# An odd unit's magnitudes ahead of the sigmoids, in the ticks that have exponentials

## The chip, the cores and the metric

The kernel runs on one core of a Trainium2 chip. The metric is device time in microseconds (us) of one execution. The engines are PE (TensorE: matmuls, with PEld for its weight loads), DVE (VectorE), ACT (ScalarE), POOL (GpSimd) and SP (SyncE, which here issues the DMAs). Each runs its own instructions in the order of the program and meets the others at semaphores.

## What is computed

Inducing-point attention over x (4 x 12480 x 128, 32 inducing rows), and then a feed-forward layer of 2048 columns with a rational function as its activation:

```
h   = mab(I, x)                      # softmax(I x^T / sqrt(C)) x
x2  = mab(x, h)                      # softmax(x h^T / sqrt(C)) h
h   = x2 @ w_in
P   = a[0] + a[1] * h + a[2] * h**2 + a[3] * h**3
Q   = 1.0 + |b[0]| * |h| + |b[1]| * h**2
out = (P / (Q + 1e-06)) @ w_out
```

## The kernel before

A first part reads x once and makes the pooled attention of the first of the 4 batches; then the weights are turned from 64-bit to 32-bit words. The main part, `fast_ticks`, walks over 832 units. A unit is one column block of 480 tokens (26 a batch) and two of the 16 slices of 128 hidden columns, so a unit's arrays are 128 x 960. One tick t stands for one unit, and the units form pairs (an even one and the odd one behind it). The later batches' attention is cut into small steps, which `side` puts between the ticks by a budget per engine when the program is built.

Q is quadratic in |h|, and with a shifted and scaled h the quotient becomes a sigmoid of a logarithm. A unit goes through these stages, with the names that the profile shows:

- `first` (L729), a tick ahead: two matmuls of 480 columns into PSUM (`hp<-at,st`). There are three `hp` buffers, so a unit's matmuls wait until the unit three before it has been read for the last time.
- The magnitude. For an even unit DVE takes it (`u<-hp`, L807). For an odd one ACT does, with an Abs (`u<-hp,all`, L821). Both halves lie in one tile `u` of 128 x 1920, so that ACT's later functions take a pair at once. There are 7 such tiles.
- The numerator's first factors: on DVE for an odd unit (`l<-u,all,hp`, L810, in the tick after it, reads the Abs), on POOL and then DVE for an even one (`l<-u,all`, L813, and `l<-hp,all,l`, L802).
- ACT: Ln over the pair (`u<-u`, L816), later Sigmoid over the pair (`u<-u,all`, L818).
- The product with the sigmoid: on DVE for an even unit (`l<-l,all,u`, L799, in tick t for unit t - 11), on POOL for the odd one behind it (`u<-l,all`, then `l<-u`, L831 and L832). POOL's first instruction writes into the half of `u` that DVE's product has just read.
- `second` (L744), 12 ticks behind: four matmuls with w_out into one PSUM tile `po`, and after eight units a column block leaves over `oT`.

Ln and Sigmoid need different tables on ACT, and a change of table is an instruction of its own (ACT_TABLE_LOAD). So the ticks run in groups of eight: with turn = (t - 6) mod 8, four Ln of four pairs in turns 0 to 3 and the four sigmoids of the same pairs in turns 4 to 7. Exponentials of the later batches' attention (`e<-e,nmc` and `a<-a`) are gathered in a queue, `exp_q`, and `run_act` lets them out in turn 4 alone, where the tables change anyhow. The table in use there for Ln is exchanged for one with the exponential first, so that such a turn has two loads: one ahead of the exponentials, one ahead of the sigmoids.

The order in which instructions are written in `fast_ticks` is the order on each engine (`InOrder`, L147, pins it). In a tick it is: matmuls of earlier and next units, DVE's and POOL's work, ACT's waiting side jobs and exponentials (`run_act`, L814), the Ln or Sigmoid of the turn, the Abs if the tick is odd (L819 to L821), and the side steps. The Abs of the odd tick behind turn 4 thus stands behind the group's second sigmoid.

Of the kernel before, what the change touches and what calls it, by code (L numbers as in the profile page):

```python
# [13 lines left out]
AF = mybir.ActivationFunctionType  # L14
# [30 lines left out]
class Params:  # L45


    def __init__(self, nc, pool, moe_a, moe_b):
        self.nc, self.pool, self.n = nc, pool, 0
        self.all = pool.tile([P, 128], F32, name="all")  # L50
        ab = pool.tile([P, 6], F32, name="ab")
        nc.sync.dma_start(out=ab[:, 0:4], in_=moe_a.rearrange("(o n) -> o n", o=1).broadcast_to((P, 4)))
        nc.sync.dma_start(out=ab[:, 4:6], in_=moe_b.rearrange("(o n) -> o n", o=1).broadcast_to((P, 2)))
        self.a = [ab[:, i:i + 1] for i in range(4)]
        self.b0 = self.abs(ab[:, 4:5])
        self.b1 = self.abs(ab[:, 5:6])
# [116 lines left out]
class Kernel:  # L173
# [50 lines left out]
    def run_act(self, exps=True):  # L224
        while self.act_q and self.act_q[0][0] < self.tick:
            _, do, done = self.act_q.pop(0)
            do()
            done.append(1)
        if exps:
            for do in self.exp_q:  # L230
                do()
            self.exp_q = []

    def run_jobs(self, spare):

        for job in list(self.jobs):
            gen, since, (ticks, v, g) = job
            if self.tick - since < ticks:
                continue
            if v > spare["v"] or g > spare["g"]:  # L240
                break
            spare["v"] -= v
            spare["g"] -= g
            need = next(gen, None)
            if need is None:
                self.jobs.remove(job)
            else:
                job[1:] = self.tick, need
# [528 lines left out]
    def fast_ticks(self, units):  # L777

        V, A, G, p = self.nc.vector, self.nc.scalar, self.nc.gpsimd, self.params
        n = len(units)
        at = lambda t: units[t] if 0 <= t < n else None
        self.first(units[0])
        for t in range(n + 13):
            u, last, d = at(t), at(t - 1), at(t - 11)
            group, turn = divmod(t - 6, 8)
            w = at(8 * group + 2 * (turn % 4))
            late = at(t - 12) and at(t - 12).key[2] == 0  # L790
            if late:
                self.fetched = self.fetch()
            if at(t - 12) and not late:
                self.second(at(t - 12))
            if at(t + 1):
                self.first(at(t + 1))
            if t % 2:
                if d:
                    V.scalar_tensor_tensor(out=d.g, in0=d.g, scalar=p.k3, in1=d.u, op0=ALU.add, op1=ALU.mult)  # L799
                    self.last_on_pool(at(t - 10), d)  # L800
                if last:
                    V.scalar_tensor_tensor(out=last.g, in0=last.h, scalar=p.k2, in1=last.g, op0=ALU.add, op1=ALU.mult)  # L802
            else:
                if u:
                    u.pair = self.mp.tile([P, 2, 2, BT], F32, tag="u", name=f"u{u.i}", bufs=7)
                    u.u = u.pair[:, 0]
                    V.tensor_scalar(out=u.u.bitcast(I32), in0=u.h.bitcast(I32), scalar1=0x7FFFFFFF, scalar2=None, op0=ALU.bitwise_and)  # L807
                if last:
                    last.g = self.new(last, "l", 14)
                    V.scalar_tensor_tensor(out=last.g, in0=last.u, scalar=p.k1, in1=last.h, op0=ALU.add, op1=ALU.mult)  # L810
                if u:
                    u.g = self.new(u, "l", 14)
                    G.tensor_scalar(out=u.g, in0=u.u, scalar1=1.0, scalar2=p.k1, op0=ALU.mult, op1=ALU.add)  # L813
            self.run_act(turn == 4)  # L814
            if w and turn < 4:
                A.activation(w.pair, w.pair, AF.Ln, bias=LAM, scale=LAM)  # L816
            elif w:
                A.activation(w.pair, w.pair, AF.Sigmoid, bias=p.lnc, scale=-2.0)  # L818
            if u and t % 2:  # L819
                u.u = last.pair[:, 1]  # L820
                A.activation(u.u, u.h, AF.Abs, bias=p.back, scale=1.0)  # L821
            self.side(u or units[-1])
            if late:
                self.second(at(t - 12))
        self.fetch()

    def last_on_pool(self, d, before):

        G, p = self.nc.gpsimd, self.params
        if d:  # L830
            G.tensor_scalar(out=before.u, in0=d.g, scalar1=1.0, scalar2=p.k3, op0=ALU.mult, op1=ALU.add)  # L831
            G.tensor_tensor(out=d.g, in0=before.u, in1=d.u, op=ALU.mult)  # L832
# [87 lines left out]
class Unit:  # L920


    def __init__(self, b, n, q):
        self.key, self.i = (b, n, q), f"{b}_{n}_{q}"


# [22 lines left out]
```

## Time and profile before

| | us |
|---|---|
| median of 3 runs | 2594.55 (2594.13 to 2599.68) |
| the profiled execution | 2594.75 |
| its span in the profile | 2592.9 |
| TensorE clock granted, mean | 0.966 of full speed |
| DMA queue 1, share of 16 engines' span | 17.6% |

Times in the profile are counted from the span's start. A page or a group's row gives busy time, mean duration and the idle time of the engine just before the group's instructions, with what released it. A row of the timeline gives start, duration, engine, line, instruction (what it writes, an arrow, what it reads) and, in brackets, the idle time before it and the releaser; neighbours of one kind are merged (x2), with their common duration. A row of the chain gives start, length and engine of a piece. All work is issued through the one helper at L157, so instructions are told apart by their tiles' names, in which buffer numbers are left out.

### The profile page before, as it was taken

What the parts mean: (1) busy time and instruction counts of PE and PEld (TensorE: products, weight loads), DVE (VectorE), ACT (ScalarE), POOL (GpSimd) and SP (SyncE); (2) the same over time, 40 slices, a digit from 0 to 9 for tenths busy, and PEclk for the clock granted to TensorE, in tenths of its full rate; (3) what the DMA queues carried; (4) which work ended last, traced back from release to release, by engine and by line L of the source; (5) the groups of instructions that cost most, each with busy time, mean ns of one, the idle gap of its engine ahead of it and who ended that gap; (6) DMA issues with size and microseconds to landing.
All of it is one profiled execution on the core that took longest, in us unless ns stands there. A gap on an engine that the chain in (4) does not pass through costs nothing.

```text
span 2592.9 us, 24006 instructions
## 1 busy us (share of the span) xinstructions
PE 2249.2 (87%) x7508; PEld 1233.8 (48%) x7508; DVE 2210.1 (85%) x2318; ACT 2244.9 (87%) x1590; POOL 2011.4 (78%) x1420
## 2 busy tenths in 40 slices
PE   7798888999899789989988898888888888888887
PEld 4544444555454355544544465444435434434333
DVE  6578778899899889899898888988889888888886
ACT  1488889989889999888899998899999999999996
POOL 2267767888787788888687887887888887888887
PEclk9699989999999999999999999999999999999999
DMA  7222201211222012112321131011101001000000
GB/s 251 73 62 78 73 27 52 71 50 31 70 83 80 19 31 76 50 48 63 92 55 48 35 88 38 16 42 31 46 27 50 27 20 38 20 22 24 17 17 17
DMA packets 117357, 133.68 MB, mean 52 GB/s; under 512 B 13544, under 2 KB 115816, under 8 KB 117224
## 3 DMA queue, kind: packets, MB, share of 16 engines
q1 hardware_dynamic: 117224, 132.06, 17.6%
q8 instruction: 64, 1.05, 0.2%
q14 instruction: 69, 0.57, 0.1%
HBM read 80.89 MB, written 25.56 MB: 41 GB/s over the span
## 4 chain that ended last, share of the span: by engine, by line
DVE 32%; PE 22%; ACT 19%; POOL 18%; issue 6%; DMA 1%; SPq 1%; DVEq 0%; POOLq 0%; ACTq 0%
DVE l L157 21%; ACT u L157 13%; POOL l L157 13%; PE po L157 13%; DVE u L157 7%; ACT L157 4%; POOL u L157 4%; PE hp L157 3%; PE ph L157 2%; PE pd L157 2%; DVE oT L157 1%; POOL a L157 1%; SPq L157 1%; DVE asm L157 1%; DMA x<-x_t 1%
## 5 line engine op out<-in xcount | busy, mean ns | idle before, releaser
L157 PE MATMUL po<-l,w_out 128*128 128x480 f32 x3328 | 1545.8, 592 | 188.4 <-POOL l L157 183.6
L157 PEld LDWEIGHTS po<-l,w_out 128*128 128x128 f32 x3328 | 607.3, 194 | 773.0 <-issue 419.7
L157 POOL TENSOR_TENSOR l<-u 128x960 f32<-128x960 f32 x416 | 932.2, 2241 | 34.7
L157 ACT ACTIVATE u<-u 128x1920 f32<-128x1920 f32 x416 | 739.8, 1799 | 193.2 <-DVE l L157 143.0
L157 PE MATMUL hp<-at,st 128*128 128x480 f32 x1664 | 742.7, 529 | 98.3 <-DVE l L157 91.1
L157 ACT ACTIVATE u<-u,all 128x1920 f32<-128x1920 f32 x416 | 766.1, 1887 | 1.2
L157 POOL TENSOR_SCALAR u<-l,all 128x960 f32<-128x960 f32 x416 | 445.5, 1071 | 392.8 <-DVE l L157 363.4
L157 DVE SCALAR_TENSOR_TENSOR l<-l,all,u 128x960 f32<-128x960 f32 x416 | 597.8, 1437 | 105.7 <-ACT u L157 105.3
L157 DVE SCALAR_TENSOR_TENSOR l<-hp,all,l 128x960 f32<-128x960 f32 x416 | 503.5, 1210 | 121.8 <-POOL l L157 114.0
L157 POOL TENSOR_SCALAR l<-u,all 128x960 f32<-128x960 f32 x416 | 555.6, 1336 | 64.7 <-DVE u L157 63.7
L157 DVE TENSOR_SCALAR u<-hp 128x960 int32<-128x960 int32 x416 | 477.0, 1147 | 75.6 <-PE hp L157 74.3
L157 PEld LDWEIGHTS hp<-at,st 128*128 128x128 f32 x1664 | 312.6, 193 | 431.3 <-issue 325.3
L157 DVE SCALAR_TENSOR_TENSOR l<-u,all,hp 128x960 f32<-128x960 f32 x416 | 500.3, 1203 | 0.3 <-ACT u L157 0.3
L157 ACT ACTIVATE u<-hp,all 128x960 f32<-128x960 f32 x416 | 434.7, 1045 | 36.4 <-PE hp L157 36.3
L157 ACT ACT_TABLE_LOAD x234 | 300.2, 1283 | 4.9 <-PEq L942 0.7
L157 PE MATMUL ph<-x,eT 120*32 120x129 f32 x832 | 105.8, 280 | 9.0 <-DMA x<-x_t 6.3
L157 PEld LDWEIGHTS pd<-HT,xTb 128*120 128x120 f32 x832 | 103.3, 198 | 9.7 <-DMA xTb<-x_c 4.3
L157 PE MATMUL pd<-HT,xTb 128*120 128x32 f32 x832 | 100.5, 277 | 5.2 <-DMA xTb<-x_c 4.1
L157 PEld LDWEIGHTS ph<-x,eT 120*32 120x32 f32 x832 | 88.9, 112 | 28.0 <-issue 21.5
L157 DVE COPY oT<-po 128x480 f32<-128x480 f32 x104 | 67.3, 647 | 21.6 <-PE po L157 21.3
L157 PE MATMUL po<-at,st 128*128 128x480 f32 x104 | 80.7, 776 | 0.0
L157 PE MATMUL pc<-xTa,ind 128*128 128x480 f32 x156 | 72.2, 566 | 1.9 <-DMA xTa<-x_c 1.9
(84 smaller groups left out, 621.6 us busy)
## 6 DMA issues: line engine op xcount, KB each, us to landing
x<-x_t SPq DMA_DIRECT2D x104, 240.0 KB, 3.5
xTb<-x_c SPq DMA_DIRECT2D x104, 240.0 KB, 2.8
at<-hl SPq DMA_DIRECT2D x416, 60.0 KB, 2.0
out<-oT SPq DMA_DIRECT2D x104, 240.0 KB, 2.0
xTa<-x_c SPq DMA_DIRECT2D x78, 240.0 KB, 2.8
xTw<-x_c SPq DMA_DIRECT2D x5, 960.0 KB, 10.3
raw<-w_in SPq DMA_DIRECT2D x4, 480.0 KB, 14.2
raw<-w_out SPq DMA_DIRECT2D x5, 384.0 KB, 5.9
```

Source lines behind the costliest of these rows:

```text
L157: ins = call(*args, **kw)
```

## The change

`run_act` now says whether it let exponentials out. If it did, the Abs of the next tick's odd unit is issued at once, behind the exponentials and ahead of the turn's sigmoid; the odd tick then leaves it out. Everywhere else the Abs stays where it was. The instruction itself moves into a method.

```
-        if exps:
-            for do in self.exp_q:
-                do()
+        todo = self.exp_q if exps else []
+        for do in list(todo):
+            do()
+        if todo:
             self.exp_q = []
+        return bool(todo)
...
-            self.run_act(turn == 4)
+            if self.run_act(turn == 4) and at(t + 1):
+                self.magnitudes(at(t + 1), u)
             if w and turn < 4:
                 A.activation(w.pair, w.pair, AF.Ln, bias=LAM, scale=LAM)
             elif w:
                 A.activation(w.pair, w.pair, AF.Sigmoid, bias=p.lnc, scale=-2.0)
-            if u and t % 2:
-                u.u = last.pair[:, 1]
-                A.activation(u.u, u.h, AF.Abs, bias=p.back, scale=1.0)
+            if u and t % 2 and u.u is None:
+                self.magnitudes(u, last)
...
+    def magnitudes(self, u, partner):
+        u.u = partner.pair[:, 1]
+        self.nc.scalar.activation(u.u, u.h, AF.Abs, bias=self.params.back, scale=1.0)
```

(`Unit` also sets `u` to None at first.)

On ACT, this is the place in the first batch where the exponential of a scores tile (`a_3`) stands in turn 4. The names give tile, column block and first slice: `hp_8_3` are the matmuls of block 8's odd unit, and `u_8_2` is the tile of its pair.

```order
 L157 ACT_TABLE_LOAD
 L157 ACTIVATE a_3_1576<-a_3_1576 120x1024
+L157 ACTIVATE u_8_2_1841<-hp_8_3_1838,all 128x960
 L157 ACT_TABLE_LOAD
 L157 ACTIVATE u_7_0_1658<-u_7_0_1658,all 128x1920
 L157 ACTIVATE u_7_2_1706<-u_7_2_1706,all 128x1920
-L157 ACTIVATE u_8_2_1841<-hp_8_3_1838,all 128x960
 L157 ACTIVATE u_7_4_1741<-u_7_4_1741,all 128x1920
 L157 ACTIVATE u_7_6_1771<-u_7_6_1771,all 128x1920
```

The Abs has passed one table load and two sigmoids. The number of rows and of table loads on ACT is the same; 26 Abs move in this way.

DVE's rows stand in the old order, but what they wait for changes. This is the group after that one, behind its turn 4, with the waits of each row; `l_9_3` is the product that reads the moved Abs, `l_8_2` the one that reads the second sigmoid.

```order
-L157 TENSOR_SCALAR u_9_4_1995<-hp_9_4_1970 128x960 [waits PE_49]
-L157 SCALAR_TENSOR_TENSOR l_9_3_1997<-u_9_2_1957,all,hp_9_3_1954 128x960 [waits Activation_49]
-L157 SCALAR_TENSOR_TENSOR l_8_2_1845<-l_8_2_1845,all,u_8_2_1841 128x960
-L157 SCALAR_TENSOR_TENSOR l_9_4_1999<-hp_9_4_1970,all,l_9_4_1999 128x960 [waits Pool_49]
+L157 TENSOR_SCALAR u_9_4_1995<-hp_9_4_1971 128x960 [waits PE_49]
+L157 SCALAR_TENSOR_TENSOR l_9_3_1997<-u_9_2_1957,all,hp_9_3_1954 128x960
+L157 SCALAR_TENSOR_TENSOR l_8_2_1845<-l_8_2_1845,all,u_8_2_1841 128x960 [waits Activation_49]
+L157 SCALAR_TENSOR_TENSOR l_9_4_1999<-hp_9_4_1971,all,l_9_4_1999 128x960 [waits Pool_49]
```

The wait for ACT has passed from the product with the Abs to the product with the second sigmoid. The product with the first sigmoid stands ahead of both and waits for ACT before and after.

More of the change, by code (lines that the diff above doesn't have):

```diff
@@ L923, in __init__ @@
     def __init__(self, b, n, q):
-        self.key, self.i = (b, n, q), f"{b}_{n}_{q}"
+        self.key, self.i, self.u = (b, n, q), f"{b}_{n}_{q}", None
 def kernel(x, inducing, moe_w_in, moe_w_out, moe_a, moe_b):
```

## The prediction

> **What bounds the kernel now.** The page's first part, and the chain that ended last by engine:
>
> ```profile
> PE 2249.2 (87%) x7508; PEld 1233.8 (48%) x7508; DVE 2210.1 (85%) x2318; ACT 2244.9 (87%) x1590; POOL 2011.4 (78%) x1420
> DVE 32%; PE 22%; ACT 19%; POOL 18%; issue 6%; DMA 1%; SPq 1%; DVEq 0%; POOLq 0%; ACTq 0%
> ```
>
> No engine is full and the chain changes hands all the time: the kernel is a ring of five engines that release one another, and a share of busy time does not say what a delay costs. So I read next who waits for whom in the groups of instructions that the change touches (busy us, mean ns, then idle time before them and its releaser):
>
> ```profile
> L157 ACT ACTIVATE u<-u 128x1920 f32<-128x1920 f32 x416 | 739.8, 1799 | 193.2 <-DVE l L157 143.0
> L157 ACT ACTIVATE u<-u,all 128x1920 f32<-128x1920 f32 x416 | 766.1, 1887 | 1.2
> L157 DVE SCALAR_TENSOR_TENSOR l<-l,all,u 128x960 f32<-128x960 f32 x416 | 597.8, 1437 | 105.7 <-ACT u L157 105.3
> L157 DVE SCALAR_TENSOR_TENSOR l<-u,all,hp 128x960 f32<-128x960 f32 x416 | 500.3, 1203 | 0.3 <-ACT u L157 0.3
> L157 ACT ACTIVATE u<-hp,all 128x960 f32<-128x960 f32 x416 | 434.7, 1045 | 36.4 <-PE hp L157 36.3
> L157 ACT ACT_TABLE_LOAD x234 | 300.2, 1283 | 4.9 <-PEq L942 0.7
> ```
>
> The rows are, in order, the Ln, the sigmoid, DVE's product with the sigmoid's output (L799), DVE's product with the odd unit's magnitudes (L810), the odd Abs and the table loads. Two rows decide the case. DVE waits 105.3 us for **sigmoids** and 0.3 us for **Abs** in the whole run. The change gives DVE the Abs sooner and the first two sigmoids later.
>
> How often: 234 loads are one at the start, 103 for Ln (the first group needs none), 104 for sigmoids, and so 26 for exponentials. The program order moves 26 Abs, one a place. Now one such place in order of time, ACT first (start, duration, instruction):
>
> ```profile
> 328.18 1.04 ACT L157 ACTIVATE u<-hp,all 128x960 f32<-128x960 f32 x1
> 329.24 1.28 ACT L157 ACT_TABLE_LOAD   x1
> 330.53 1.10 ACT L157 ACTIVATE e<-e,nmc 128x960 f32<-128x960 f32 x1
> 331.64 1.28 ACT L157 ACT_TABLE_LOAD   x1
> 332.94 3.68 ACT L157 ACTIVATE u<-u,all 128x1920 f32<-128x1920 f32 x2
> 336.53 1.04 ACT L157 ACTIVATE u<-hp,all 128x960 f32<-128x960 f32 x1
> 337.47 3.67 ACT L157 ACTIVATE u<-u,all 128x1920 f32<-128x1920 f32 x2
> ```
>
> The Abs that moves is the one at 336.53; it goes to 331.6, ahead of the load at 331.64. The other engines there (the row at 339.88 is the product with the second sigmoid):
>
> ```profile
> 329.20 0.96 PE L157 MATMUL hp<-at,st 128*128 128x480 f32 x2
> 334.87 1.22 DVE L157 SCALAR_TENSOR_TENSOR l<-l,all,u 128x960 f32<-128x960 f32 x1 [2.18 <-ACT u L157]
> 336.19 1.07 POOL L157 TENSOR_SCALAR u<-l,all 128x960 f32<-128x960 f32 x1 [3.81 <-DVE l L157]
> 339.88 1.71 DVE L157 SCALAR_TENSOR_TENSOR l<-l,all,u 128x960 f32<-128x960 f32 x1
> 337.36 0.66 PE L157 MATMUL hp<-at,st 128*128 128x480 f32 x2 [3.45 <-DVE l L157]
> ```
>
> DVE stands 2.18 us for the first sigmoid, and POOL (3.81) and PE (3.45) stand for DVE. Everything is stopped behind that one sigmoid. The chain through this group, from the load to the group's third Ln (a piece of DVE, PE or POOL each time the releaser changes), and that Ln's own wait:
>
> ```profile
> 331.64 1.28 ACT L157
> 332.94 1.91 ACT u L157
> 334.87 1.23 DVE l L157
> 336.19 1.08 POOL u L157
> 337.34 2.23 POOL l L157
> ...
> 353.20 1.13 DVE l L157
> 354.42 2.76 ACT u L157 x2
> ```
> ```profile
> 354.42 1.80 ACT L157 ACTIVATE u<-u 128x1920 f32<-128x1920 f32 x1 [2.52 <-DVE l L157]
> ```
>
> It goes from the sigmoid over DVE, POOL, PE and DVE back into ACT, and ACT waits 2.52 us at its end. So a late first sigmoid is handed round the ring to the next group.
>
> **The change part by part.** *Removed:* the Abs behind the second sigmoid. Started at 336.53, it held the next sigmoid until 337.47, so 0.94 us: two ACTIVATEs overlap by 0.10. *Added:* the same Abs behind the exponentials. It overlaps the exponential in the same way, so it can start 1.00 after the exponential's start at 330.53; the next table load follows an Abs by 1.06 (328.18 to 329.24), while it followed the exponential by 1.11 (330.53 to 331.64). First and second sigmoid are therefore late by 1.00 + 1.06 - 1.11 = **0.95 us**; the third gets 0.94 back and is on time. No load, no DMA and no instruction is added or dropped: the order shows the same 234 loads, and ACT issues no DMA that would be moved past. The Ln's and DVE's changed semaphore lists I put at nothing: a wait whose event is long past shows no idle time (the sigmoids' 1.2 us over 416).
>
> *The added wait:* the Abs reads the `hp` of the next odd unit. In the place above its matmuls end at 329.20 + 0.96 = 330.16, before the exponential's end, and Abs does not wait. That holds at 19 of 26. At 7 the matmuls end after the exponential; the first and the last of the 7:
>
> ```profile
> 150.17 0.63 ACT L157 ACTIVATE a<-a 120x512 f32<-120x512 f32 x1
> 151.45 0.97 PE L157 MATMUL hp<-at,st 128*128 128x480 f32 x2
> ...
> 1422.80 1.09 ACT L157 ACTIVATE e<-e,nmc 128x960 f32<-128x960 f32 x1
> 1424.70 0.97 PE L157 MATMUL hp<-at,st 128*128 128x480 f32 x2
> ```
>
> There 152.42 - 150.80 = 1.62 and 1425.67 - 1423.89 = 1.78 (1.77 unrounded); between them lie 1.43, 1.01, 0.04, 0.21 and 1.41, together 7.49 us. Behind the waiting Abs the whole of ACT is queued: load, four sigmoids, next Abs; and DVE, POOL and PE wait for the first of those. How soon Abs follows such matmuls:
>
> ```profile
> 348.07 0.97 PE L157 MATMUL hp<-at,st 128*128 128x480 f32 x2
> 349.14 1.06 ACT L157 ACTIVATE u<-hp,all 128x960 f32<-128x960 f32 x1 [1.78 <-PE hp L157]
> ```
>
> 0.10 us behind their end. So at a late place the first sigmoid is late by the wait + 0.10 + 1.06, less the 0.01 that the load already stood behind the exponential: wait + 1.15.
>
> *What hides it:* nothing, where DVE already waits for that sigmoid. It does so at all 26; the first and the last:
>
> ```profile
> 154.04 1.22 DVE L157 SCALAR_TENSOR_TENSOR l<-l,all,u 128x960 f32<-128x960 f32 x1 [1.50 <-ACT u L157]
> ...
> 2194.66 1.22 DVE L157 SCALAR_TENSOR_TENSOR l<-l,all,u 128x960 f32<-128x960 f32 x1 [2.73 <-ACT u L157]
> ```
>
> The 26 waits run from 1.18 to 3.58 us and make 63.3 of the 105.7. The second sigmoid, late as well, is needed by DVE only at 339.88 in the place above, 3.3 us after its old end of 332.94 + 3.68 = 336.62: covered. The gain, a sooner Abs, is at most the 0.3 us of its row.
>
> *The sum:* 19 x 0.95 = 18.1; 7 x 1.15 + 7.49 = 15.5; together **33.6 us**, to which the 0.3 at most is a gain I neglect. Of this, how much is handed on? At 21 of the 26 places the chain leaves ACT for DVE at the first sigmoid, as above: all of it. At 5 it stays on ACT for all four sigmoids, as here:
>
> ```profile
> 306.78 5.61 ACT u L157 x4
> ...
> 316.00 1.08 POOL u L157
> ```
>
> There only the third sigmoid's lateness counts for certain, and the rest if DVE has no slack; bounds per place are 0.01 and 0.95, 4.7 us for the five. I take the full value, the one that the 21 others have: DVE stood for the first sigmoid at these five too, so its own row of work starts that much later. The profiled execution took 2594.75 us (span 2592.9 and 1.85 around it), 0.2 from the median of 2594.55. So 2594.75 + 33.6 = **2628**; 2623.6 with the five at their low bound.
>
> A rule to weigh here. From the end of the exponential at 331.63 to the sigmoid at 332.94 the rows have 1.31 us, the load and next to nothing. The Trainium skill (ScalarE: Activation LUTs, What ACT_TABLE_LOAD costs) gives a switch about 1283 ns for the load and about 1380 ns more for a drain, 2.66 us in all; were there such a drain behind the exponential, Abs could run in it, and the sum would keep only the late matmuls. The load's length agrees; the drain is not in these rows, and the rows decide.
>
> **The rivals.** *Handed on in part* (10%). DVE is 85% busy, so between two exchanges it could catch up; the chain's 6% of "issue" may hide slack that I count as none. Half of 33.6 is 16.8: 2611.6. Against it: POOL's and PE's waits above are caused by DVE's.
>
> *ACT is the bound* (6%). Its 87% is the highest that counts pure work. The moved Abs leaves ACT's work the same, and the third sigmoid moves by 0.01, or by wait + 0.21 where the matmuls are late: 19 x 0.01 + 7 x 0.21 + 7.49 = 9.2, so 2603.9. Against it are the 193.2 us in which ACT stands before Ln. (The Trainium skill, Perfetto Trace Analysis, Identifying the Most-Contended Engine, takes the engine of the highest occupancy for the one to work on and warns of matmul time; by that rule this rival would be the forecast. Here the chain has ACT at 19%, DVE at 32%.)
>
> *Not slower: it is swallowed before the Ln* (6%). ACT idles up to some 2.5 us before the group's third Ln. If that wait is ended by work which does not come from the first sigmoid, then lateness below it vanishes: 2594.8, and at most 0.3 less. It decides where the idle time exceeds 0.95, or the wait + 0.21 at a late place, and where the chain into that Ln does not pass the first sigmoid. Against it: in the group shown it does pass.
>
> *Worse* (4%). Late groups make later `hp` matmuls late against the exponentials, so that more than 7 places wait: were all 26 to wait the 1.07 us that the 7 average, 26 x (1.15 + 1.07) = 57.7, so 2652. Against it: in the place shown the matmuls end 1.5 us ahead of the exponential, more than one place adds.
>
> That the move does not take place is excluded by the order.
>
> **How the numbers follow.** The forecast has 74%. 0.2%, or 5.2 us, is about what a measurement of this kernel can tell from no change. Of the swallowed case I put 2% to faster and 4% to within 0.2%; all others are slower, 94%. The range runs from below the half case, 2610, to 2640, some way into the last one; outside stay ACT as the bound, the swallowed case and most of the worst, under 16%, and some error of the forecast itself.
>
> **What would show it.** In the changed profile: 26 Abs between exponential and load, the Abs group's idle time behind `hp` up from 36.3 by some 8 us; DVE's idle time before the sigmoid products up from 105.7 by about 30, that of POOL and PE behind DVE at these places by about 1 us each; the first sigmoid 2.3 us (before: 1.3) behind the exponential's end; ACT busy unchanged at 2245; the Ln's idle time up by some 20. The forecast is wrong if the span grows by much less than DVE's wait for sigmoids does (swallowed, or handed on in part), or if the first sigmoid comes later than by 0.95 us at most places (worse).

## The result, and the profile after

The changed kernel takes 2632.9 us (median of 4 runs, 2631.97 to 2633.79), the one before 2596.02 beside it: a ratio of **1.0140, 95% interval 1.0123 to 1.0158**, so 1.4% slower, 36 us of 2596 (32 to 41 by the interval). The forecast was 2628, with a range of 2610 to 2640.

The same groups as before, on the page of the changed kernel (busy us, mean ns, then idle time before them and its releaser):

```profile
PE 2264.0 (86%) x7508; PEld 1241.0 (47%) x7508; DVE 2205.2 (84%) x2318; ACT 2246.7 (85%) x1590; POOL 2010.1 (76%) x1420
L157 ACT ACTIVATE u<-u 128x1920 f32<-128x1920 f32 x416 | 739.9, 1799 | 213.9 <-DVE l L157 153.1
L157 DVE SCALAR_TENSOR_TENSOR l<-l,all,u 128x960 f32<-128x960 f32 x416 | 593.9, 1428 | 138.2 <-ACT u L157 137.8
L157 DVE SCALAR_TENSOR_TENSOR l<-u,all,hp 128x960 f32<-128x960 f32 x416 | 500.0, 1202 | 0.3 <-ACT u L157 0.3
L157 ACT ACTIVATE u<-hp,all 128x960 f32<-128x960 f32 x416 | 435.0, 1046 | 55.4 <-PE hp L157 53.4
```

ACT does the same work (2244.9 before, 2246.7 now). The product with the Abs still waits 0.3 us in the whole run: the change gave DVE nothing sooner that it had been waiting for. The product with the sigmoid waits 137.8 us for ACT instead of 105.3: 32.5 us more. Who waited for that product in turn, in the view of the waits (total us, times, longest), first in the kernel before and then in the changed one:

```profile
POOL u L157 <- DVE l L157: 363.4, 252, 4.0
PE hp L157 <- DVE l L157: 91.1, 77, 3.6
```
```profile
POOL u L157 <- DVE l L157: 398.9, 254, 5.8
PE hp L157 <- DVE l L157: 124.8, 81, 5.0
```

POOL has 35.5 us more, PE 33.7. The place that the prediction showed, now in order of time, first ACT, then DVE, POOL and PE:

```profile
335.52 1.10 ACT L157 ACTIVATE e<-e,nmc 128x960 f32<-128x960 f32 x1
336.52 1.04 ACT L157 ACTIVATE u<-hp,all 128x960 f32<-128x960 f32 x1
337.58 1.28 ACT L157 ACT_TABLE_LOAD   x1
338.88 7.25 ACT L157 ACTIVATE u<-u,all 128x1920 f32<-128x1920 f32 x4
```
```profile
340.81 1.22 DVE L157 SCALAR_TENSOR_TENSOR l<-l,all,u 128x960 f32<-128x960 f32 x1 [2.30 <-ACT u L157]
342.12 1.07 POOL L157 TENSOR_SCALAR u<-l,all 128x960 f32<-128x960 f32 x1 [3.93 <-DVE l L157]
343.30 0.74 PE L157 MATMUL hp<-at,st 128*128 128x480 f32 x1 [3.81 <-DVE l L157]
```

From the exponential's start to the first sigmoid it is 338.88 - 335.52 = 3.36 us; before it was 332.94 - 330.53 = 2.41. The difference is the 0.95 that the sum used. The first of the seven places with late matmuls:

```profile
148.39 0.63 ACT L157 ACTIVATE a<-a 120x512 f32<-120x512 f32 x1
150.74 1.06 ACT L157 ACTIVATE u<-hp,all 128x960 f32<-128x960 f32 x1 [1.72 <-PE hp L157]
...
149.68 0.97 PE L157 MATMUL hp<-at,st 128*128 128x480 f32 x2
```

Here the Abs stands 1.72 us for PE, and the load and all four sigmoids stand behind it.

### The profile page after: what moved, and what is told of

The parts are those of the page before. It is cut to its first block, busy times and chain, and to the rows that moved or that the text cites. A ratio compares the mean times of both kernels' runs of the same rounds, so it can differ in the third digit from the quotient of the medians.

```text
span 2631.4 us, 23981 instructions
## 1 busy us (share of the span) xinstructions
PE 2264.0 (86%) x7508; PEld 1241.0 (47%) x7508; DVE 2205.2 (84%) x2318; ACT 2246.7 (85%) x1590; POOL 2010.1 (76%) x1420
## 4 chain that ended last, share of the span: by engine, by line
DVE 30%; PE 27%; POOL 18%; ACT 17%; issue 5%; DMA 2%; SPq 1%; POOLq 0%; DVEq 0%; ACTq 0%
DVE l L157 20%; PE po L157 16%; POOL l L157 12%; ACT u L157 12%; DVE u L157 6%; PE hp L157 4%; POOL u L157 4%; ACT L157 4%; PE ph L157 3%; PE pd L157 2%; DVE oT L157 1%; SPq L157 1%; PE pc L157 1%; POOL a L157 1%; DVE asm L157 1%
## 5 line engine op out<-in xcount | busy, mean ns | idle before, releaser
L157 PEld LDWEIGHTS po<-l,w_out 128*128 128x128 f32 x3328 | 614.6, 196 | 775.4 <-issue 430.8
L157 ACT ACTIVATE u<-u 128x1920 f32<-128x1920 f32 x416 | 739.9, 1799 | 213.9 <-DVE l L157 153.1
L157 PE MATMUL hp<-at,st 128*128 128x480 f32 x1664 | 743.9, 529 | 132.5 <-DVE l L157 124.8
L157 DVE SCALAR_TENSOR_TENSOR l<-l,all,u 128x960 f32<-128x960 f32 x416 | 593.9, 1428 | 138.2 <-ACT u L157 137.8
L157 ACT ACTIVATE u<-hp,all 128x960 f32<-128x960 f32 x416 | 435.0, 1046 | 55.4 <-PE hp L157 53.4
L157 DVE COPY oT<-po 128x480 f32<-128x480 f32 x104 | 67.2, 646 | 21.6 <-PE po L157 21.2
```

The source lines that it names most:

```text
L157: ins = call(*args, **kw)
```

## The experiments

All kernels ran with the one before beside them on the same chip; ratios are against it, in brackets the 95% interval. Not all ran on one chip, so two kernels of different sections are compared by their ratios.

### The Abs behind the first sigmoid

The Abs still moves, but by one sigmoid only: the first sigmoid is back on time and the second is late. Against the changed kernel:

```
-            if self.run_act(turn == 4) and at(t + 1):
-                self.magnitudes(at(t + 1), u)
+            ran = self.run_act(turn == 4)
...
                 A.activation(w.pair, w.pair, AF.Sigmoid, bias=p.lnc, scale=-2.0)
+            if ran and at(t + 1):
+                self.magnitudes(at(t + 1), u)
```

> The 26 Abs move up by one sigmoid only, behind the first of the group instead of behind the second. Theory (the first sigmoid's lateness is what costs): that sigmoid is on time, only the second is late by 0.94 us, and it had 3.3 us to spare; the time stays that of before, 2593 to 2599 us. Rival (any earlier Abs costs, because ACT's queue or DVE's waits are set otherwise, or the second sigmoid's lateness is handed on): 26 x 0.94, so 2615 to 2625.

Measured: 2591.67 us, ratio 0.9995 (0.9985 to 1.0004), 1.3 us below the range, with the kernel before at 2593.47 beside it. The same place, ACT and then DVE, and DVE's product over the whole run:

```profile
330.44 1.28 ACT L157 ACT_TABLE_LOAD   x1
331.73 1.90 ACT L157 ACTIVATE u<-u,all 128x1920 f32<-128x1920 f32 x1
333.53 1.04 ACT L157 ACTIVATE u<-hp,all 128x960 f32<-128x960 f32 x1
334.48 5.46 ACT L157 ACTIVATE u<-u,all 128x1920 f32<-128x1920 f32 x3
```
```profile
333.66 1.22 DVE L157 SCALAR_TENSOR_TENSOR l<-l,all,u 128x960 f32<-128x960 f32 x1 [2.45 <-ACT u L157]
337.55 1.21 DVE L157 SCALAR_TENSOR_TENSOR l<-u,all,hp 128x960 f32<-128x960 f32 x1
338.68 1.71 DVE L157 SCALAR_TENSOR_TENSOR l<-l,all,u 128x960 f32<-128x960 f32 x1
```
```profile
L157 DVE SCALAR_TENSOR_TENSOR l<-l,all,u 128x960 f32<-128x960 f32 x416 | 596.6, 1435 | 105.7 <-ACT u L157 105.3
```

The second sigmoid now ends about 334.48 + 1.9 = 336.4, and its product begins at 338.68 without idle time before it: covered. The Abs ends at 334.57 and its product begins at 337.55, so that a sooner Abs was of no use either. DVE waits 105.3 us for sigmoids, as in the kernel before. Moving the Abs is free; moving it ahead of the *first sigmoid* costs the 1.4%.

### Only the late places, and only the others

The change at a part of its places, again against the changed kernel:

```
-            if self.run_act(turn == 4) and at(t + 1):
+            if self.run_act(turn == 4) and at(t + 1) and group in (1, 4, 9, 22, 47, 51, 53):
```

with `group not in` in the second kernel (the numbers count the groups of eight ticks).

> The Abs moves ahead of the sigmoids' load only at the 7 places where the matmuls of its unit ended after the exponential in the trace of before; at the other 19 it stays. Theory: 7 x 1.15 + 7.49 = 15.5 us slower than before, 2610 to 2614. Rival (the wait for the matmuls is covered, only the order on ACT counts): 7 x 0.95 = 6.7 us slower, 2602 to 2604.

> The complement: the Abs moves at the 19 places where the matmuls were done, and stays at the 7. Theory: 19 x 0.95 = 18.1 us slower than before, 2612 to 2617, with the 7 adding up to the whole change. Rival (the cost is nearly all in the waits for late matmuls): under 4 us slower, 2596 to 2600.

Measured: the 7 late places alone 2615.1 us, ratio 1.0078 (1.0056 to 1.0100), 20 us (15 to 26); the 19 others alone 2609.61 us, ratio 1.0071 (1.0051 to 1.0090), 18 us (13 to 23). Together 38.6, the whole change within its interval. The two medians lie just outside the ranges on record, the first 1.1 us above and the second 2.4 below; against the kernel before, both intervals hold their sums (15.5 and 18.1). The rows that answer, the sigmoid's product of the late places' kernel and then of the other's:

```profile
L157 DVE SCALAR_TENSOR_TENSOR l<-l,all,u 128x960 f32<-128x960 f32 x416 | 592.9, 1426 | 121.1 <-ACT u L157 120.6
```
```profile
L157 DVE SCALAR_TENSOR_TENSOR l<-l,all,u 128x960 f32<-128x960 f32 x416 | 596.9, 1435 | 123.1 <-ACT u L157 122.8
```

15.3 and 17.5 us above the 105.3 of before: 15.5 and 18.1 were the sums. Seven places cost as much as nineteen, because the wait for PE's matmuls comes on top: both rivals, which dropped one of the two terms, are out.

### The other direction: a load less ahead of the first sigmoid

The kernel before, with one table that holds Ln and Exp, loaded at each group's first Ln. The exponentials then need no load of their own.

```
             if w and turn < 4:
+                if turn == 0:
+                    A.preload_act_table_set("natural_log_exp_and_others")
                 A.activation(w.pair, w.pair, AF.Ln, bias=LAM, scale=LAM)
```

> The kernel before, with the table that holds both Ln and Exp loaded for each group's Ln, so that the exponentials need no load of their own: 209 loads instead of 234, and the first sigmoid of the 26 places comes 1.30 us sooner, without any Abs moved. Theory (whatever stands ahead of that sigmoid is paid in full by the whole ring): 26 x 1.30 = 33.8 us faster, 2560 to 2566. Rival (ACT has idle time enough, or the next engine in the ring takes over as soon as the sigmoid is less late): 0 to 15 us faster, 2581 to 2596.

Measured: 2562.54 us, ratio 0.9888 (0.9870 to 0.9906): 29 us faster (24 to 34). ACT at the same place, and DVE's row:

```profile
318.10 1.04 ACT L157 ACTIVATE u<-hp,all 128x960 f32<-128x960 f32 x1
319.05 1.08 ACT L157 ACTIVATE e<-e,nmc 128x960 f32<-128x960 f32 x1
320.14 1.28 ACT L157 ACT_TABLE_LOAD   x1
321.44 3.69 ACT L157 ACTIVATE u<-u,all 128x1920 f32<-128x1920 f32 x2
```
```profile
323.37 1.22 DVE L157 SCALAR_TENSOR_TENSOR l<-l,all,u 128x960 f32<-128x960 f32 x1 [0.76 <-ACT u L157]
```

The exponential follows the Abs without a load, and DVE's wait falls from 2.18 to 0.76. The Ln takes 1799 ns in both kernels, so the other table does not make it faster. What stands ahead of the first sigmoid is paid in both directions.

### The joint table and the change together

The changed kernel, with the same table edit:

```
             if w and turn < 4:
+                if turn == 0:
+                    A.preload_act_table_set("natural_log_exp_and_others")
                 A.activation(w.pair, w.pair, AF.Ln, bias=LAM, scale=LAM)
```

> The joint table and the change together: the Abs behind the exponentials as in the changed kernel, and no load ahead of them. The exponentials then end 1.30 us sooner against PE, so the Abs waits for its matmuls at nearly all 26 places: taken from the trace of before with each exponential's end 1.30 us sooner, the waits and the 1.15 (or 0.95) a place make 60 us. Theory (an Abs ahead of the sigmoids hands PE's lateness to the whole ring): 2562 + 60 = 2622, 2612 to 2628. Rival (the change costs a fixed time on ACT, whatever stands around it): 2562 + 37 = 2599, 2592 to 2604.

Measured: 2623.88 us, ratio 1.0110 (1.0093 to 1.0126). Against the joint table alone that is 1.0110 / 0.9888 = 1.0225, 58 us on 2563, where the change on its own cost 36. The Abs group's idle time is up:

```profile
L157 ACT ACTIVATE u<-hp,all 128x960 f32<-128x960 f32 x416 | 435.6, 1047 | 77.9 <-PE hp L157 75.3
```

75.3 us for PE, 34.2 in the joint table alone and 53.4 in the changed kernel; the moved Abs alone wait 29.1 us at the 26 places, where in the changed kernel it is 6.6 us. The same edit costs more once the work ahead of it is shorter, since it ties the sigmoids to PE; a fixed price on ACT, the rival, is out.

### Exponentials ahead of the fourth Ln

ACT waits for DVE there, 2.16 us at the place shown above in the joint table's trace. To the joint table's kernel comes:

```
-            self.run_act(turn == 4)
+            self.run_act(turn == 3)
```

> The kernel with the joint table for Ln and Exp (209 loads), and the exponentials let out one turn sooner: ahead of the group's fourth Ln, where ACT waits for DVE, so that only a table load stands between the last Abs and the first sigmoid. Theory (what stands ahead of the first sigmoid is paid, what stands in ACT's idle time before the fourth Ln is not): a further 0.6 to 1.1 us at each of some 26 places, 15 to 28 us below the 2562 of the joint table alone, 2534 to 2548. Rival (ACT's idle time there is used up, the exponential delays the Ln instead): 2558 to 2565.

Measured: 2566.25 us, ratio 0.9887 (0.9871 to 0.9904): no gain over the joint table, though DVE's wait for sigmoids fell by another 21.6 us. The product's row in the joint table's kernel, then in this one, and this one's fourth Ln at the place:

```profile
L157 DVE SCALAR_TENSOR_TENSOR l<-l,all,u 128x960 f32<-128x960 f32 x416 | 593.3, 1427 | 74.7 <-ACT u L157 74.2
```
```profile
L157 DVE SCALAR_TENSOR_TENSOR l<-l,all,u 128x960 f32<-128x960 f32 x416 | 594.2, 1429 | 53.4 <-ACT u L157 52.6
317.87 1.08 ACT L157 ACTIVATE e<-e,nmc 128x960 f32<-128x960 f32 x1
320.13 1.81 ACT L157 ACTIVATE u<-u 128x1920 f32<-128x1920 f32 x1 [1.18 <-DVE l L157]
```

The time is the rival's (1.3 us above its range), but its reason is not seen at this place: behind the exponential the Ln still waits 1.18 us for DVE. This kernel also lets `side` see the exponentials a turn sooner, and so its steps of attention fall into other ticks; seven of the 26 places lie a group later than in the joint table's kernel. The 33 groups with exponentials in either kernel take 12 to 26 us less in its trace, by where a group is cut, and the others 13 to 28 more: what is gained in the one is lost in the other. So a second kernel emitted those exponentials that were ready in turn 3, and told the side steps of them in turn 4: DVE, PE, POOL and SP have the joint table's order row for row.

```
-        if exps:
-            for do in self.exp_q:
-                do()
+        if exps == "early":
+            self.held += [do() for do in self.exp_q]
             self.exp_q = []
+        elif exps:
+            held, self.held = self.held + [do() for do in self.exp_q], []
+            self.exp_q = []
+            for done in held:
+                done()
...
-            self.run_act(turn == 4)
+            self.run_act({3: "early", 4: True}.get(turn))
```

> The joint table, with the exponentials that are ready let out ahead of the group's fourth Ln, but with their completion told to the side steps one turn later, so that DVE, PE, POOL and SP have row for row the order of the joint table alone and only some 20 exponentials move on ACT. It asks why the run with all exponentials moved gained nothing. Theory (the exponentials ahead of the fourth Ln are nearly free, and that run lost the gain elsewhere, to side steps that were put in other ticks): about 1 us at each of some 19 places, ratio 0.978 to 0.985 against before, 2537 to 2555. Rival (the rest of DVE's wait for the first sigmoid is not worth anything any more, since another engine bounds the group): a ratio of 0.987 to 0.990, 2560 to 2568.

Measured: 2556.62 us, ratio 0.9851 (0.9829 to 0.9874), between the two expectations and close to the theory's upper end. By the ratios that is about 10 us better than the joint table alone, half of what the theory gave; the two intervals overlap slightly (0.9870 and 0.9874). It is the fastest of these kernels, 1.5% below the one before. In its trace DVE's waits for the first sigmoid of the 26 places add up to 23.5 us, against 34.0 in the joint table's. At three of them, the one shown above with 0.76 us among them, that wait is gone, and at that place the chain stays on DVE's own work, so that a still sooner sigmoid would gain nothing there. That the rest went to the side steps' new ticks in the first kernel fits the two runs, but is not shown beyond the 10 us.

### Matmuls to fill PE's pauses

The changed kernel, with extra matmuls whose results nothing reads, in the time in which PE stands behind the late sigmoid.

```
             if at(t + 1):
                 self.first(at(t + 1))
+            if t == self.fill:
+                for _ in range(14):
+                    self.nc.tensor.matmul(self.po[:, BT:512], self.st[u.key[0]][:, 0:P], u.rhs[:, 0:32], start=True, stop=True)
...
             if self.run_act(turn == 4) and at(t + 1):
                 self.magnitudes(at(t + 1), u)
+                self.fill = t + 1
```

> The changed kernel with 14 extra matmuls of 32 columns at each of the 26 places, into 32 columns of a PSUM tile that nothing reads, in the time in which PE stands behind the late sigmoid. It asks where the change's few us beyond the first sigmoid's lateness come from. Theory (PE's longer pauses bring half-clock intervals of 3.4 us behind them, which slow matmuls on the chain): with the pauses partly filled, fewer such intervals than the 39 of the changed kernel and 3 to 10 us less than its 1.014 against before, a ratio of 1.010 to 1.013. Rival (the intervals do not come from the pauses, or do not cost): intervals as many as before, ratio 1.013 to 1.016.

Measured: 2628.89 us, ratio 1.0143 (1.0120 to 1.0166), beside the change's 1.0140. The pauses were filled in part (PE's wait for DVE before `hp` fell from 124.8 to 89.1 us). By the traces' clock records, one execution each, the half-clock intervals went from 39 (212 us) to 36 (185 us), against 35 (178 us) in the kernel before, and the mean granted clock rose from 0.960 to 0.965. So there are fewer intervals, as the theory had it, but the time did not follow: by that it is the rival's. The ratio's interval of 12 us is wider than the effect sought, so the run decides little.

## Why the prediction was right

**The frequency and the order** (26 Abs, ahead of the load) are as the prediction had them. Where it spoke of the group's third Ln, at 354.42, it is the fourth: two came as one row at 343.86. Nothing in the sum rests on that.

**0.95 us a place** is what the rows show (3.36 against 2.41), and the 19 such places alone cost 18 us against 18.1.

**The waits for late matmuls** were forecast at 7.49 us in 7 places, and 1.15 more for each. The first has 1.72 us of idle time where 1.62 + 0.10 was forecast. The 7 alone made DVE wait 15.3 us longer against 15.5. One of them, the last, all but vanished in the changed kernel: its matmuls came 0.1 us after the exponential instead of 1.77. So the seven were not seven fixed numbers, and the joint table with the change shows how far they can move. The sign for the whole Abs group was missed: its idle time behind PE rose by 17.1 us (36.3 to 53.4), where 8 was forecast. The moved Abs make 6.6 of it; the rest stands before Abs that had not moved (at 167, 467 and 657 us, for example), a cost that the sum does not have.

**Handed on in full.** DVE's wait grew by 32.5 us (forecast: about 30), and the time by 36 (32 to 41). The five places where the chain stayed on ACT were rightly taken at their full value. From the start of their group's fourth Ln, where the chain comes back into ACT, to that of the next group's, they take together 8.6 us longer in the changed trace; at full value they stood in the sum with 8.0, at the low bound with 3.3. The rival *handed on in part* (2611.6), *ACT is the bound* (2603.9) and *swallowed before the Ln* (2594.8) are all outside the measured runs. The 19 places without late matmuls rule out the second of these by themselves: there the third sigmoid moves by 0.01 us, and the cost was 18 us. The rival *worse* had the mechanism of the joint table with the change, but not in this kernel, where most matmuls were done in time.

**What the sum left out.** It gave 33.6 and DVE's extra wait is 32.5, while the profiled execution grew by 38.5 in its span (2592.9 to 2631.4). By the interval of the timed runs the sum could be exact. From fourth Ln to fourth Ln, the 26 groups with a moved Abs take 35.3 us longer in the changed trace, the other groups 5.1 longer, and the part ahead of the first one 1.9 less (cut at DVE's instructions near the fourth Ln, the first two come out the same within 1.3). That 35.3 lies so near to 33.6 is in part luck: the group of the last late place took 1.7 us less than forecast, since its wait all but vanished, and other groups with a moved Abs made up for it. A stretch without any moved Abs can take 3.8 us longer, as the kernel with the late places alone shows (the last section). Whether the change brings such stretches about, or chance put them there, stays open: the run that filled PE's pauses did not settle it.

## What to carry to other kernels

When engines release one another in a ring, look up which instruction the others are standing for at the place of the edit, and keep everything from ahead of it; an instruction for which nobody waits (here 0.3 us in 416) gains nothing by being sooner, whatever it passes on its way. Moving an instruction up an in-order queue also moves its own wait up: everything behind it then waits for its producer, and that price grows when the work ahead of it gets shorter. And the same wait shows where to cut: taking a table load from ahead of that sigmoid won 29 us, where putting an Abs there lost 36. But a shorter wait is not always a shorter run: with all exponentials ahead of the fourth Ln, DVE's wait fell by 21.6 us and the time stayed.

## What was not expected of the hardware

With the same work, a stretch can take longer because the granted TensorE clock halves for a while. This is the view by stretches of time (length, then busy us and instructions of PE, PEld, DVE, ACT and POOL, then the granted clock, DMA's share and GB/s) from the end of one place's exponential to that of the next, first in the kernel before, then in the one with the late places alone, where no Abs has moved in it:

```profile
604.65:680.62 75.97, 68.52 (x277) 41.19 (x276) 65.95 (x62) 65.53 (x46) 58.51 (x39) 0.98 0.18 56
```
```profile
611.70:691.50 79.80, 72.55 (x277) 43.40 (x276) 65.92 (x62) 65.58 (x47) 58.42 (x39) 0.91 0.17 53
```

The same 277 matmuls take 3.8 us longer, and the other engines' work is unchanged. Inside it stand eight `po` matmuls behind a pause of 2.6 us, again before and then after; the nearest moved Abs ahead of them lies some 280 us back:

```profile
636.85 0.63 PE L157 MATMUL pa<-ident,a 120*128 120x120 f32 x4 [2.63 <-POOL a L157]
637.31 3.39 PE L157 MATMUL po<-l,w_out 128*128 128x480 f32 x8
```
```profile
643.87 1.06 PE L157 MATMUL pa<-ident,a 120*128 120x120 f32 x4 [2.60 <-POOL a L157]
644.72 5.91 PE L157 MATMUL po<-l,w_out 128*128 128x480 f32 x8
```

3.39 us became 5.91. The view by stretches for that piece:

```profile
637.00:641.00 4.00, 4.00 (x15) 2.24 (x15) 2.02 (x2) 3.97 (x5) 3.92 (x3) 1.00 0.46 97
```
```profile
643.00:649.80 6.80, 5.93 (x11) 3.16 (x12) 3.05 (x3) 6.77 (x6) 6.04 (x4) 0.50 0.40 100
```

A pause of the same length (2.63 and 2.60 us) was followed by full clock in the one and by half clock in the other. The clock records of the traces (when the granted clock changed) tell the two apart. In each of the ten traces all half-clock intervals begin on one grid with a step of 3.41 us, and last one or more whole steps (the last one may be cut off by the trace's end). This is the step of that grid in which most of the pause lies, before and then after:

```profile
635.01:638.43 3.42, 1.58 (x7) 1.05 (x8) 2.79 (x3) 3.42 (x4) 3.42 (x3) 1.00 0.52 143
```
```profile
639.54:642.95 3.41, 1.37 (x6) 0.56 (x4) 3.41 (x4) 3.41 (x4) 3.33 (x3) 1.00 0.26 88
```

PE is busy for 1.58 us of the step in the one, and the next step has full clock; for 1.37 us in the other, and the next step has half. Over the ten traces, from 130 us on, each of the 178 steps at full clock in which PE was busy for under 0.42 of the step, by the profile's rows, was followed by half clock, and of the 6537 with 0.53 or more only 35 were; in between it went either way (60 of 144). These bounds describe these traces and were not tested by a run of their own. The Trainium skill (TensorE: Matmul & The Clock Gate, Part 1: The HAM clock gate) tells of an activity window of 3.4 us that runs freely, so that the moment at which the clock rises depends on where in the window the first matmul lands; the grid agrees with that. So where a pause falls on the grid counts as well as its length, and two kernels' spans can differ by some us for a reason that has nothing to do with the edit.
